# Scores of two heads in one task, FFN tiles moved by 32 bytes, warm matmuls in another bank

## The chip, the cores and the metric

The kernel runs on one core of a Trainium2 chip. The metric is the device time of one execution in microseconds (us): the median of three runs.

## The reference

Windowed attention with four sink positions feeds two FFN layers. Shapes: batch 2, 8 heads, 768 tokens, head size 64; the FFNs map 1536 tokens of width 512 through 2048 hidden columns and back.

```
scores = q @ k.T / sqrt(64)
keep   = (key < n_sink) | (0 <= query - key < window)      # n_sink = 4, window = 128
a      = softmax(where(keep, scores, -1e9))
x      = (a @ v), heads side by side -> (1536, 512)
h = x @ w1_in;  g = h if h >= 1, 0 if h <= -1, else (h + 1)**2 / 4;  x = g @ w1_out
h = x @ w2_in;  out = relu(h)**2 @ w2_out
```

The inputs arrive as 64-bit numbers; the output is float32.

## The kernel before

**Attention** is cut into 24 units (`UNITS`): batch b, block j of 256 queries, pair c of two heads. The name of a tile carries them: `s_0_2_1_1_0` is the score tile of unit (b 0, j 2, c 1), query half u = 1, head e = 0. A unit goes through these tasks: `tp` (TensorE turns k and q into bank `tp`) and `tpc` (VectorE copies them to `k`), `s` (TensorE: scores of one head and one half, 260 keys wide, 128 in a sequence's first half), `m` (VectorE adds the mask and takes the least, L668, which frees the score bank), `e` (ScalarE's exponential), `n`, `pm`, `sp` (normalizing, VectorE and GpSimd), `x` and `ts` (TensorE turns the weights; ScalarE copies), `av` (TensorE, weights times values), `xh` and `xl` (the result, split in two float32r parts, goes to the big tile `x`).

A score matmul contracts over the 64 rows of one head: head 0 uses rows 0 to 63 of TensorE, head 1 rows 64 to 127. The scores have two PSUM banks (`SCB = 2`), one tile each.

**The FFN** works in passes over chunks of 128 hidden columns. Weights come from HBM by SyncE's queue, are split in two float32r parts by ScalarE, VectorE and GpSimd (`wx`, `wy`, `w`), and lie in nine slots of 8 KB per partition: slots 0 to 5 stand on the left side of SBUF, beside `x`; slots 6 to 8 stand on the right side and open when attention is over. Chunks take the slots in turn. A hidden step is twelve matmuls (L357, tile `h`, moving operand `x`, stationary `w`), an output step is three matmuls for each chunk of the pass (L425, tile `o`; in the first FFN `g` moves and `w` is stationary, in the second `w` moves and `g` is stationary). A piece of 256 tokens is taken while attention still runs (`STEPS`, passes 0 and 1), one of 512 later. The later `g` tiles are on the right side too.

**Places.** `fill` puts a tile in front of the FFN's tiles so that they start at a multiple of `LINE` = 2048 bytes. It reckons with `BOTTOM`, the bytes that the pools `one` and `first` take. They take 11,328 bytes, and `BOTTOM` says 11,296: so the left tiles stand 32 bytes behind a multiple of 2048 (the built program has `x` at byte 61,472 and weight slot 0 at 12,320). The right side's weight slots and `g` tiles stand at multiples of 512 (slot 6 at 219,136).

**The order** of all instructions from the fast path on is a list made when the kernel is built: `Planner.run` takes the task that can start first by its table of costs, and among those that can start at once the one with the least key (`KEYS`, `STEPS`, `LOADS`, `PARTS`). Each engine works through its part of the list in order. Where the planner leaves TensorE idle before the first FFN matmul, `warm_gaps` puts matmuls of the identity (`warm_c`). `warm_pe` does the same by hand at the start: `warm_a`, `warm_b` and `warm_d`, around the sum that spreads the parameters over the partitions (`par_ps`, L233, bank `psf0`), whose copy is `par_all` (L241).

Of the kernel before, what the change touches and what calls it, by code (L numbers as in the profile page):

```python
# [8 lines left out]
F32 = mybir.dt.float32  # L9
# [8 lines left out]
P = 128  # L18
# [10 lines left out]
SCALE = 0.125  # L29
BIG = 8.0e9  # L30
GRP = 2
WARM = 3, 3, 1
VB, KB = 5, 6
PB, PTB = 6, 4
WR = 2
UNITS = [(b, j, c) for b in range(B) for j in range(3) for c in range(NC)]
RING, EARLY = 9, 6
G0, G1 = 7, 6
LINE, BOTTOM, TOP, DMA_SCRATCH = 2048, 11296, 229344, 1024
PSF, SCB, TPB, TXB = 2, 2, 1, 2  # L40
HALF = 256
SLOTS = dict(
    q=2, v=VB, k=KB, p=PB, pt=PTB, sm=4, sp=2, st=2, vs=1, av=2, sc=SCB, tp=TPB, tx=TXB, f=PSF,
# [1 line left out]
)  # L45
LATE = dict(f=8 - PSF, w=RING - EARLY, G=G1, U=2, T=2)
KEYS = dict(
    q=-82.12, v=149.88, kd=-59.27, kp=-207.24, tp=115.34, tpc=40.08, kp0=-0.30, s0=1.56,
    m0=-62.00, e0=130.89, s1=2.49, m1=-159.82, e1=180.50, n=27.64, pm0=296.62, sp0=-106.62,
    pm1=-268.00, sp1=11.63, x0=-230.35, xc0=-85.23, x1=-6.43, xc1=106.04, ts=-154.44, tsc=122.15,  # L50
    tsl=3.21, av=207.79, xh=-0.06, xl=-291.84, vs=94.69, vc=-27.99, k1=102.40, k2=-128.71,
)
STEPS = [
    (0, 0, 157.84), (0, 256, -39.25), (0, 512, 13.62), (1, 512, 52.44), (0, 1024, -5.62),
    (1, 0, 59.36), (1, 256, 63.06), (1, 1024, 135.44), (0, 768, 23.61), (1, 768, 394.12),
    (0, 1280, 34.67), (1, 1280, 129.91),
]
SPREAD = 21.09, 3.72
LOADS = [-36.47, 48.25, 302.68, -2.39, -160.55, 14.45]
PARTS = [170.15, 9.91, -52.22, 170.63, -252.48, 135.47]  # L60
START = dict(SP=4900.0, PE=6500.0, ACT=6900.0, DVE=5900.0, POOL=5700.0)
LEAD = 153.00, 55.20
LAG = dict(PE=53, ACT=33, DVE=33, POOL=78, SP=40)
COST = dict(
    q=("SP", 2200, 0, 2320), v=("SP", 1100, 0, 1160), kd=("SP", 500, 0, 230), wi=("SP", 500, 0, 1470),
# [2 lines left out]
    pm=("POOL", 1012, 1060, 0), pms=("POOL", 562, 615, 0), sp=("POOL", 139, 203, 0),  # L68
    cl=("POOL", 1235, 1275, 0), gl=("POOL", 690, 740, 0), gl5=("POOL", 1240, 1290, 0),
    yl=("POOL", 690, 740, 0), yl5=("POOL", 1240, 1290, 0),  # L70
    tp=("PE", 436, 620, 0), s=("PE", 320, 389, 0), ss=("PE", 207, 285, 0), x=("PE", 436, 633, 0),
    xx=("PE", 327, 490, 0), ts=("PE", 218, 400, 0), av=("PE", 1230, 1390, 0), avv=("PE", 790, 870, 0),
    mm=("PE", 120, 283, 0), mm5=("PE", 226.7, 390, 0),
    e=("ACT", 500, 510, 0), es=("ACT", 392, 400, 0), xc=("ACT", 492, 587, 0), xxc=("ACT", 375, 478, 0),
# [44 lines left out]
class Planner:  # L119
# [28 lines left out]
    def switch(self, last, t):  # L148
        if last is None or t.engine != "PE":
            return 0.0  # L150
        if t.kind in ("s", "ss"):
            return 0.0 if last.kind in ("s", "ss") else 90.0
        if last.kind in TURNS:
            return 50.0 if t.kind in TURNS else -80.0
        return 0.0
# [407 lines left out]
class Attention:  # L563
# [84 lines left out]
            blocks = slice(4 * i // len(ps), 4 * (i + 1) // len(ps))  # L648
            copy(self.kt[b, j, c][:, 1:, :P][:, blocks], ps[i][:, blocks])  # L649

    def scores(self, b, j, c, u, e):
        nc, po, st = self.nc, self.po, self.st[b, j, c]
        kt = self.kt[b, j, c]
        keys = kt.rearrange("p n w -> p (n w)")
        k0 = SLOT if (j == 0 or u == 1) else 0
        wid = P if j + u == 0 else WIN
        ps = st["s", u, e] = po["sc"].tile([P, 512], F32, tag="s", name=f"s_{st['nm']}_{u}_{e}")[:, :wid]
        pr = slice(64 * e, 64 * e + 64)
        nc.tensor.matmul(ps, kt[pr, 3 + u, :P], keys[pr, k0 : k0 + wid], start=True, stop=True)  # L659

    def least(self, b, j, c, u, e):
        nc, po, st = self.nc, self.po, self.st[b, j, c]
# [101 lines left out]
    def plan(self, line):  # L764
        add, hold = line.add, Hold
        raw, val, keyh, sinks, self.mask_tasks = {}, {}, {}, {}, {}
        u = {}
        for n, unit in enumerate(UNITS):
            b, j, c = unit
            old = u.get((b, j - 1, c))  # L770
            d = u[unit] = {}
            at = lambda f, *a, t=unit: (lambda: f(*t, *a))
            key = lambda nm, n=n: n + KEYS[nm]
            if (j, c) == (0, 0):
                h, sinks[b, 0] = hold("pt"), hold("vs")
                uses = ([h], []), ([], []), ([sinks[b, 0]], []), ([], []), ([], [h])
                last = None
                for i, (kind, f) in enumerate(self.sinks(b)):
                    at0 = n + KEYS["vs"] if i < 2 else n + KEYS["vc"] + 0.01 * i
                    last = add(kind, at0, f, [last], *uses[i])  # L780
                sinks[b] = last
            g = (b, j, c // 2)
            if c % 2 == 0:
                if n:
                    raw[g] = hold("q")
                    d["q"] = add("q", key("q"), at(self.loads.load, "qk"), takes=[raw[g]])
                val[g] = hold("v")
                d["v"] = add("v", key("v"), at(self.loads.load, "v"), takes=[val[g]])
            else:
                d["q"], d["v"] = u[b, j, c - 1].get("q"), u[b, j, c - 1]["v"]  # L790
            kt = keyh[unit] = hold("k")
            if j > 0:
                d["kd"] = add(
                    "kd", key("kd"), at(self.keys_load), [old["tpc"]], [kt], [keyh[b, j - 1, c]]
                )
                d["kp"] = add(
                    "kp", key("kp"), at(self.keys_sink), [d["kd"], old["kp"]], [], [keyh[b, j - 1, c], kt]
                )
            if n:
                h = hold("tp")  # L800
                t = add("tp", key("tp"), at(self.turn), [d["q"]], [h], [raw[g]] if g in raw else [])
                d["tpc"] = add(
                    "tpc", key("tpc"), at(self.turn_copy), [t], [] if j else [kt], [h, kt],
                    behind=d.get("kd"),
                )
            else:
                kt.pool = "none"
                d["tpc"] = None
            if j == 0:
                d["kp"] = add("kp0", key("kp0"), at(self.keys_sink), [d["tpc"]], [], [kt])  # L810
            ph, sm, exps = [hold("p"), hold("p")], hold("sm"), []
            for i in range(2):
                small = "s" if j + i == 0 else ""
                for e in range(2):
                    least = None if i + e == 0 else least
                    h = hold("sc")
                    t = add(
                        "s" + small, key(f"s{i}") + 0.001 * e, at(self.scores, i, e),
                        [d["tpc"], d["kp"], d.get("kd")], [h], [kt],
                    )  # L820
                    t = add(
                        "m" + small, key(f"m{i}") + 0.001 * e, at(self.least, i, e),
                        [t, self.mask_of(line, min(2 * j + i, 2))], [ph[i]] * (e == 0) + [sm] * (i + e == 0),
                        [h], behind=least,
                    )
                    least = t
                    exps.append(add("e" + small, key(f"e{i}") + 0.001 * e, at(self.powers, i, e), [t]))
            norm = add("n", key("n"), at(self.norm), exps)
            pm, cols = [], []
            sp, stt, av = hold("sp"), hold("st"), hold("av")  # L830
            for i in range(2):
                small = "s" if j + i == 0 else ""
                pm.append(add("pm" + small, key(f"pm{i}"), at(self.weigh, i), [norm], [], [sm]))
                if j > 0:
                    cols.append(
                        add("sp", key(f"sp{i}"), at(self.sink_cols, i), [pm[-1]], [sp][i:], [ph[i]])
                    )
            turned, ptu = [], []
            few = "x" if j == 0 else ""
            for e in range(2):  # L840
                h, pt = hold("tx"), hold("pt")
                t = add(few + "x", key(f"x{e}"), at(self.turn_p, e), pm, [h], ph)
                turned.append(add(few + "xc", key(f"xc{e}"), at(self.turn_p_copy, e), [t], [pt], [h]))
                ptu.append(pt)
            if j > 0:
                h = hold("tx")
                t = add("ts", key("ts"), at(self.turn_s), cols, [h], [sp])
                t = add("tsc", key("tsc"), at(self.turn_s_copy), [t], [stt], [h])
                turned.append(add("tsl", key("tsl"), at(self.turn_s_low), [t], [], [h]))
# [378 lines left out]
def attention_ffn_kernel(ctx, tc, q, k, v, n_sink, window, w1i, w1o, w2i, w2o, out):  # L1228
    nc = tc.nc
# [14 lines left out]
    with tc.manual_schedule(engines={mybir.EngineType.DVE, mybir.EngineType.PE}):  # L1244
# [3 lines left out]
        masks = Masks(nc, one, par)  # L1248
        par.compute(psf[0], masks.m[2][0:1, :P])
        masks.begin()  # L1250
        warm_pe(nc, ident, psf, "b", WARM[1])
        at.turn(*UNITS[0])
        at.turn_copy(*UNITS[0])
        masks.first()
# [40 lines left out]
```

## Time and profile before

| | |
|---|---|
| median of three runs | 671.44 us (670.66 to 671.64) |
| the profiled execution | 671.85 us |
| its span, first to last instruction | 670.1 us |
| TensorE busy | 655.4 us, 98% |
| VectorE, ScalarE, GpSimd busy | 438.6, 331.1, 299.7 us |
| mean granted TensorE clock | 0.994 |

The profiled execution takes 1.75 us more than its span. Attention's last matmuls run at about 178 us; from there to the end there is FFN alone. TensorE counts as busy from a matmul's start to its modelled end, with the ends of neighbours overlapping, so 98% busy does not say that nothing is lost.

### The profile page before, as it was taken

What the parts mean: (1) busy time and instruction counts of PE and PEld (TensorE: products, weight loads), DVE (VectorE), ACT (ScalarE), POOL (GpSimd) and SP (SyncE); (2) the same over time, 40 slices, a digit from 0 to 9 for tenths busy, and PEclk for the clock granted to TensorE, in tenths of its full rate; (3) what the DMA queues carried; (4) which work ended last, traced back from release to release, by engine and by line L of the source; (5) the groups of instructions that cost most, each with busy time, mean ns of one, the idle gap of its engine ahead of it and who ended that gap; (6) DMA issues with size and microseconds to landing.
All of it is one profiled execution on the core that took longest, in us unless ns stands there. A gap on an engine that the chain in (4) does not pass through costs nothing.

```text
span 670.1 us, 9926 instructions
## 1 busy us (share of the span) xinstructions
PE 655.4 (98%) x3550; PEld 536.8 (80%) x3550; DVE 438.6 (65%) x906; ACT 331.1 (49%) x720; POOL 299.7 (45%) x314
## 2 busy tenths in 40 slices
PE   8998999989999999999999999999999999999997
PEld 6575777878999988888888888888888888888885
DVE  4877899876668587676777687666666566622222
ACT  3777877865455444344445555533544444412220
POOL 3447565556144253344444697433543444323311
PEclk9998999999999999999999999999999999999999
DMA  6664641211021123221121122222212211100011
GB/s 150 170 155 110 146 131 41 81 63 33 3 93 64 33 64 94 64 64 63 64 81 50 58 64 64 63 64 69 88 63 72 86 64 64 32 1 31 32 63 70
DMA packets 63904, 47.95 MB, mean 72 GB/s; under 512 B 39652, under 2 KB 58340, under 8 KB 63844
## 3 DMA queue, kind: packets, MB, share of 16 engines
q1 hardware_dynamic: 62466, 46.56, 23.8%
q10 hardware_dynamic: 1378, 0.66, 0.3%
q8 instruction: 30, 0.49, 0.3%
q14 instruction: 30, 0.25, 0.1%
HBM read 43.01 MB, written 3.15 MB: 69 GB/s over the span
## 4 chain that ended last, share of the span: by engine, by line
PE 95%; DVE 2%; ACT 1%; issue 1%; POOL 0%; POOLq 0%; DVEq 0%
PE h L357 40%; PE o L425 40%; PE s L659 5%; PE av L747 3%; PE tx L706 3%; PE tp L635 2%; DVE p L668 1%; PE warm_c L866 1%; PE ts L719 1%; DVE k L649 1%; ACT p L676 0%; ACT pt L713 0%; PE warm_b L866 0%; PE warm_a L866 0%; DVE wx L299 0%
## 5 line engine op out<-in xcount | busy, mean ns | idle before, releaser
L357 PE MATMUL h<-x,w 128*128 128x512 f32 (+1 forms) x1368 | 279.1, 359 | 0.2 <-DVE acc L462 0.2
L357 PEld LDWEIGHTS h<-x,w 128*128 128x128 f32 x1368 | 229.7, 189 | 41.5 <-DVE t L371 0.8
L301 POOL TENSOR_TENSOR w<-wx,w 128x512 fp32r<-128x512 f32 x64 | 83.4, 1303 | 146.7 <-ACT w L300 134.1
L425 PE MATMUL o<-g,w 128*128 128x256 f32 (+1 forms) x792 | 142.5, 335 | 1.2 <-DVE acc L462 1.2
L425 PEld LDWEIGHTS o<-g,w 128*128 128x128 f32 x792 | 120.7, 190 | 19.4 <-DVE acc L462 2.3
L425 PE MATMUL o<-w,g 128*128 128x512 f32 (+1 forms) x588 | 135.6, 389 | 0.0
L425 PEld LDWEIGHTS o<-w,g 128*128 128x128 f32 x588 | 108.8, 188 | 25.1
L382 POOL TENSOR_TENSOR g<-t,g 128x512 fp32r<-128x512 f32 x48 | 63.7, 1327 | 91.3 <-ACT g L378 65.9
L382 POOL TENSOR_TENSOR g<-u,g 128x256 fp32r<-128x256 f32 (+1 forms) x66 | 71.7, 1092 | 70.0 <-ACT g L378 61.8
L464 DVE TENSOR_TENSOR acc<-o,acc 128x512 f32<-128x512 f32 (+1 forms) x109 | 59.8, 563 | 62.4 <-PE o L425 62.2
L373 DVE SCALAR_TENSOR_TENSOR t<-h,u 128x512 f32<-128x512 f32 x48 | 33.1, 689 | 71.4 <-ACT u L366 43.1
L300 ACT CAST w<-wx 128x512 fp32r<-128x512 f32 x64 | 39.8, 621 | 79.2 <-DVE wx L299 79.1
L371 DVE SCALAR_TENSOR_TENSOR t<-u 128x256 f32<-128x256 f32 (+1 forms) x66 | 46.7, 708 | 27.8 <-ACT u L364 27.4
L690 POOL TENSOR_TENSOR p<-p,sm 128x520 f32<-128x520 f32 (+1 forms) x48 | 49.1, 1034 | 33.1 <-DVE sm L683 19.2
L289 DVE SCALAR_TENSOR_TENSOR wx<-wraw,wx 128x512 int32<-128x512 int32 x64 | 62.4, 975 | 1.3
L279 ACT ACTIVATE wx<-wraw 128x512 f32<-128x512 f32 x64 | 42.7, 667 | 38.1 <-POOL w L301 38.0
L364 ACT ACTIVATE u<-h,half 128x256 f32<-128x256 f32 (+1 forms) x66 | 37.3, 569 | 47.3 <-PE h L357 38.3
L366 ACT ACTIVATE u<-h 128x512 f32<-128x512 f32 x48 | 28.5, 594 | 52.9 <-PE h L357 50.9
L676 ACT ACTIVATE p<-p,sm 128x260 f32<-128x260 f32 (+1 forms) x96 | 46.7, 488 | 14.2 <-DVE sm L668 13.9
L299 DVE CUSTOM_DVE_ANT_0 wx<-wx,wy 128x1024 uint16<-128x1024 uint16 x64 | 50.6, 790 | 2.3
L378 ACT CAST g<-u 128x256 fp32r<-128x256 f32 (+1 forms) x66 | 32.7, 501 | 29.5 <-DVE u L389 19.7
L659 PE MATMUL s<-k 64*128 64x260 f32 (+1 forms) x192 | 42.2, 437 | 4.9 <-DVE sm L668 4.8
(79 smaller groups left out, 574.1 us busy)
## 6 DMA issues: line engine op xcount, KB each, us to landing
wraw<-in_moe_w_in_dram SPq DMA_DIRECT2D x32, 512.0 KB, 3.8
wraw<-in_moe_w_out_dram SPq DMA_DIRECT2D x32, 512.0 KB, 3.2
vr<-in_v_dram SPq DMA_DIRECT2D x24, 128.0 KB, 2.7
qr<-in_q_dram SPq DMA_DIRECT2D x22, 128.0 KB, 2.5
kr<-in_k_dram SPq DMA_DIRECT2D x22, 128.0 KB, 3.1
out_dram<-acc SPq DMA_DIRECT2D x10, 256.0 KB, 2.1
k<-k SPq DMA_DIRECT2D x16, 64.0 KB, 2.3
qr<-in_q_dram SPq DMA_DIRECT2D x4, 64.0 KB, 2.4
```

The source lines that it names most:

```text
L279: nc.scalar.activation(s["x"], f32(s["r"][:, :, 1]), AF.Abs, scale=65536.0)
L289: nc.vector.scalar_tensor_tensor(s["xi"], s["r"][:, :, 1], -(1 << 31), s["xi"], ALU.bitwise_and, ALU.bitwise_or)
L299: ("c4", lambda: nc.vector.tensor_tensor(s["xi"], s["xi"], s["yi"], ALU.add)),
L301: ("cl", lambda: nc.gpsimd.tensor_tensor(s["w"][:, 1], s["x"], f32(s["w"][:, 0]), ALU.subtract)),
L357: nc.tensor.matmul(s["h"], w[:, a, c * P : (c + 1) * P], x[:, b, c, sl], start=n == 0, stop=n == 11)
L371: nc.vector.scalar_tensor_tensor(t, s["u"], 1.0, s["u"], ALU.min, ALU.mult)
L382: nc.gpsimd.tensor_tensor(g[:, 1], s["u" if ffn == 0 else "t"], f32(g[:, 0]), ALU.subtract)
L425: nc.tensor.matmul(s["o"], lhs, rhs, start=n + i + j == 0, stop=n == len(chunks) - 1 and i == 1)
L464: self.nc.vector.tensor_tensor(dst, o, dst, ALU.add)
L659: nc.tensor.matmul(ps, kt[pr, 3 + u, :P], keys[pr, k0 : k0 + wid], start=True, stop=True)
L676: self.nc.scalar.activation(s, s, AF.Exp, bias=sm[:, 0, u, e : e + 1], scale=-1.0, accum_out=sm[:, 1, u, e : e + 1])
L690: self.nc.gpsimd.tensor_tensor(s, s, r, ALU.mult)
```

## The change

Four things are changed. The scores of both heads of a query half are one task, which takes both score banks at once. `BOTTOM` is 11,328, so that the left FFN tiles move 32 bytes down, to multiples of 2048 (`x` to 61,440, slot 0 to 12,288). The matmuls `warm_b` write `psf[1:]`, so bank `psf1` alone, and `WARM` has one less of them and one more `warm_d`. All keys of the planner are other numbers, and the score's cost is that of two.

```diff
-WARM = 3, 3, 1
+WARM = 3, 2, 2
-LINE, BOTTOM, TOP, DMA_SCRATCH = 2048, 11296, 229344, 1024
+LINE, BOTTOM, TOP, DMA_SCRATCH = 2048, 11328, 229344, 1024
-    q=-82.12, v=149.88, kd=-59.27, kp=-207.24, tp=115.34, tpc=40.08, kp0=-0.30, s0=1.56,
+    q=-128.99, v=155.46, kd=-117.16, kp=-232.79, tp=110.17, tpc=65.09, kp0=31.66, s0=-3.92,
...
-    (0, 0, 157.84), (0, 256, -39.25), (0, 512, 13.62), (1, 512, 52.44), (0, 1024, -5.62),
+    (0, 0, 100.20), (0, 256, -58.54), (0, 512, 27.88), (1, 512, 156.32), (1, 0, 42.56),
...
-    tp=("PE", 436, 620, 0), s=("PE", 320, 389, 0), ss=("PE", 207, 285, 0), x=("PE", 436, 633, 0),
+    tp=("PE", 436, 620, 0), s=("PE", 640, 709, 0), ss=("PE", 415, 492, 0), x=("PE", 436, 633, 0),
...
-    def scores(self, b, j, c, u, e):
+    def scores(self, b, j, c, u):
...
-        ps = st["s", u, e] = po["sc"].tile([P, 512], F32, tag="s", name=f"s_{st['nm']}_{u}_{e}")[:, :wid]
-        pr = slice(64 * e, 64 * e + 64)
-        nc.tensor.matmul(ps, kt[pr, 3 + u, :P], keys[pr, k0 : k0 + wid], start=True, stop=True)
+        for e in range(2):
+            ps = po["sc"].tile([P, 512], F32, tag="s", name=f"s_{st['nm']}_{u}_{e}")[:, :wid]
+            st["s", u, e] = ps
+            pr = slice(64 * e, 64 * e + 64)
+            nc.tensor.matmul(ps, kt[pr, 3 + u, :P], keys[pr, k0 : k0 + wid], start=True, stop=True)
...
-                for e in range(2):
-                    least = None if i + e == 0 else least
-                    h = hold("sc")
-                    t = add(
-                        "s" + small, key(f"s{i}") + 0.001 * e, at(self.scores, i, e),
-                        [d["tpc"], d["kp"], d.get("kd")], [h], [kt],
-                    )
+                hs = [hold("sc"), hold("sc")]
+                first = add(
+                    "s" + small, key(f"s{i}"), at(self.scores, i),
+                    [d["tpc"], d["kp"] if j + i else None, d.get("kd")], hs, [kt],
+                )
+                for e, h in enumerate(hs):
...
-        warm_pe(nc, ident, psf, "b", WARM[1])
+        warm_pe(nc, ident, psf[1:], "b", WARM[1])
```

On TensorE, at the program's start, the rows of before, with the semaphores that each waits for (DVE is VectorE, DMAHW a load's landing, PE TensorE's own):

```order
L233 MATMUL par_ps_112<-par_val_110,mask2_102 128x2 [waits DVE_49,PE_49]
L866 MATMUL warm_b_0_125<-ident_67 128x128 [waits DVE_49]
L866 MATMUL warm_b_1_127<-ident_67 128x128
L866 MATMUL warm_b_2_129<-ident_67 128x128 [waits PE_49]
L635 MATMUL tp_0_0_0_0_131<-ident_67,kr_0_0_0_78 128x128 [waits DMAHW3_49,PE_49]
```

and of the change:

```order
L233 MATMUL par_ps_112<-par_val_110,mask2_102 128x2 [waits DVE_49,PE_49]
L867 MATMUL warm_b_0_125<-ident_67 128x128
L867 MATMUL warm_b_1_127<-ident_67 128x128 [waits PE_49]
L635 MATMUL tp_0_0_0_0_129<-ident_67,kr_0_0_0_78 128x128 [waits DMAHW3_49,DVE_49]
L635 MATMUL tp_0_0_0_0_129<-ident_67,kr_0_0_0_78 128x128 [waits DMAHW5_49]
```

The first `warm_b` no longer waits for VectorE's copy, and the first `tp` no longer waits for the warm matmuls' writes.

On TensorE, in the third block of queries of batch 0, the rows of before from the last score of unit (0, 1, 3) on:

```order
L659 MATMUL s_0_1_3_1_1_849<-k_0_1_3_446 128x260
L659 MATMUL s_0_2_0_0_0_851<-k_0_2_0_536 128x260
L659 MATMUL s_0_2_0_0_1_861<-k_0_2_0_536 128x260
L659 MATMUL s_0_2_0_1_0_865<-k_0_2_0_536 128x260
L635 MATMUL tp_1_0_1_0_871<-ident_67,kr_1_0_0_659 128x128 x2
L635 MATMUL tp_1_0_1_0_871<-ident_67,qr_1_0_0_656 128x128 x2
L659 MATMUL s_0_2_0_1_1_882<-k_0_2_0_536 128x260
L659 MATMUL s_0_2_1_0_0_893<-k_0_2_1_547 128x260
L659 MATMUL s_0_2_1_0_1_902<-k_0_2_1_547 128x260
L659 MATMUL s_0_2_1_1_0_906<-k_0_2_1_547 128x260
```

and of the change, from the first score of unit (0, 2, 0) on:

```order
L661 MATMUL s_0_2_0_0_0_865<-k_0_2_0_499 128x260
L661 MATMUL s_0_2_0_0_1_867<-k_0_2_0_499 128x260
L708 MATMUL tx_0_1_2_1_873<-ident_67,p_0_1_2_0_701 128x128 x2
L708 MATMUL tx_0_1_2_1_873<-ident_67,p_0_1_2_1_732 128x128 x2
L661 MATMUL s_0_2_0_1_0_888<-k_0_2_0_499 128x260
L661 MATMUL s_0_2_0_1_1_890<-k_0_2_0_499 128x260
L749 MATMUL av_261<-sink_t0_264,vs_0_438 128x256
```

Scores now stand in pairs of heads of the same half, with turns, `av` and FFN steps (`h_0_0_1`, twelve matmuls, two pairs further down) between the pairs; before, four scores of two different pairs follow each other.

## Rows read from the trace of the kernel before

**Rows 1.** The page: TensorE's busy time, and the chain that ended last, by engine.

```profile
PE   655.4 (98%) x3550; PEld 536.8 (80%) x3550; DVE 438.6 (65%) x906; ACT 331.1 (49%) x720; POOL 299.7 (45%) x314
PE 95%; DVE 2%; ACT 1%; issue 1%; POOL 0%; POOLq 0%; DVEq 0%
```

**Rows 2.** Stretches of attention: busy us (instructions) by engine, granted clock, DMA.

```profile
16.40:41.70 25.30, 23.64 (x171) 16.10 (x171) 19.51 (x70) 19.43 (x62) 12.70 (x24) 1.00 0.75 183
41.70:60.80 19.10, 17.23 (x112) 11.29 (x111) 16.18 (x55) 15.18 (x47) 11.12 (x20) 1.00 0.51 130
60.80:67.70 6.90, 6.90 (x34) 5.24 (x33) 3.25 (x9) 3.39 (x10) 5.29 (x8) 0.51 0.18 42
67.70:120.00 52.30, 50.39 (x396) 39.54 (x395) 47.52 (x146) 40.92 (x123) 30.06 (x43) 1.00 0.42 110
120.00:180.00 60.00, 58.10 (x469) 49.35 (x468) 42.77 (x119) 39.11 (x104) 28.93 (x39) 1.00 0.14 41
```

**Rows 3.** The chain in order of time, second FFN: start us, us, what.

```profile
466.21 10.89 PE h L357 x48
477.10 11.19 PE o L425 x48
...
576.78 11.13 PE h L357 x48
587.91 11.04 PE o L425 x48
```

**Rows 4.** Groups by line and shape: FFN matmuls 512 wide, count, busy us, mean ns.

```profile
L357 PE MATMUL h<-x,w 128*128 128x512 f32 x936 | 219.4, 391 | 0.0
L425 PE MATMUL o<-w,g 128*128 128x512 f32 x564 | 132.8, 394 | 0.0
L425 PE MATMUL o<-g,w 128*128 128x512 f32 x360 | 85.9, 394 | 0.0
```

**Rows 5.** TensorE, program start: start us, us, line, tile, records [idle before].

```profile
3.41 0.58 PE L233 MATMUL par_ps<-par_val,mask 1*128 1x2 f32 x2
4.25 1.65 PE L866 MATMUL warm_b<-ident 128*128 128x128 f32 x6 [0.25 <-DVE par_all L241]
5.96 0.69 PE L635 MATMUL tp<-ident,kr 128*128 128x128 f32 x2
...
7.98 0.80 PE L659 MATMUL s<-k 64*128 64x128 f32 x4
```

**Rows 6.** Line L659, the scores: what ended idle time before them (us, times).

```profile
  DVE sm L668: 13.5, 26
```

**Rows 7.** TensorE in order of time: a pair of heads alone, then two pairs running.

```profile
69.01 0.71 PE L659 MATMUL s<-k 64*128 64x260 f32 x4
69.65 0.38 PE L747 MATMUL av<-sink_t,vs 96*128 96x256 f32 x1
...
143.51 0.71 PE L659 MATMUL s<-k 64*128 64x260 f32 x4
144.75 1.05 PE L659 MATMUL s<-k 64*128 64x260 f32 x4 [0.52 <-DVE sm L668]
145.73 0.39 PE L747 MATMUL av<-sink_t,vs 96*128 96x256 f32 x1
```

**Rows 8.** TensorE in order of time, 50 to 66 us: the third block's scores.

```profile
50.92 1.05 PE L659 MATMUL s<-k 64*128 64x260 f32 x4 [0.52 <-DVE sm L668]
...
55.33 0.70 PE L659 MATMUL s<-k 64*128 64x260 f32 x2
55.96 1.09 PE L706 MATMUL tx<-ident,p 128*128 128x128 f32 x8
...
60.58 1.58 PE L659 MATMUL s<-k 64*128 64x260 f32 x4 [0.68 <-DVE sm L668]
62.09 1.11 PE L706 MATMUL tx<-ident,p 128*128 128x128 f32 x4
...
65.57 1.63 PE L357 MATMUL h<-x,w 128*128 128x256 f32 x6
```

More of the change, by code (lines that the diff above doesn't have):

```diff
@@ L47 @@
 KEYS = dict(
-    q=-82.12, v=149.88, kd=-59.27, kp=-207.24, tp=115.34, tpc=40.08, kp0=-0.30, s0=1.56,
-    m0=-62.00, e0=130.89, s1=2.49, m1=-159.82, e1=180.50, n=27.64, pm0=296.62, sp0=-106.62,
-    pm1=-268.00, sp1=11.63, x0=-230.35, xc0=-85.23, x1=-6.43, xc1=106.04, ts=-154.44, tsc=122.15,
-    tsl=3.21, av=207.79, xh=-0.06, xl=-291.84, vs=94.69, vc=-27.99, k1=102.40, k2=-128.71,
+    q=-128.99, v=155.46, kd=-117.16, kp=-232.79, tp=110.17, tpc=65.09, kp0=31.66, s0=-3.92,
+    m0=-102.11, e0=252.45, s1=-3.31, m1=-67.76, e1=276.89, n=56.38, pm0=592.38, sp0=-61.87,
+    pm1=-212.96, sp1=89.25, x0=-220.28, xc0=-249.08, x1=-19.51, xc1=50.14, ts=-99.41, tsc=98.15,
+    tsl=42.27, av=248.63, xh=6.01, xl=-352.66, vs=28.63, vc=-54.27, k1=-185.94, k2=-176.52,
 )
 STEPS = [
-    (0, 0, 157.84), (0, 256, -39.25), (0, 512, 13.62), (1, 512, 52.44), (0, 1024, -5.62),
-    (1, 0, 59.36), (1, 256, 63.06), (1, 1024, 135.44), (0, 768, 23.61), (1, 768, 394.12),
-    (0, 1280, 34.67), (1, 1280, 129.91),
-]
[L58 to L62, printed above, removed]
+    (0, 0, 100.20), (0, 256, -58.54), (0, 512, 27.88), (1, 512, 156.32), (1, 0, 42.56),
+    (0, 1024, 124.89), (1, 256, 68.66), (1, 1024, 281.52), (0, 768, -15.98), (1, 768, 400.16),
+    (0, 1280, -3.57), (1, 1280, 161.21),
+]
+SPREAD = 26.48, 15.61
+LOADS = [13.24, -77.84, 364.45, -42.84, -98.01, -150.31]
+PARTS = [78.66, 20.27, -1.00, 151.41, -446.58, 123.12]
+START = dict(SP=4100.0, PE=6400.0, ACT=6400.0, DVE=5950.0, POOL=6500.0)
+LEAD = 197.30, 93.66
 LAG = dict(PE=53, ACT=33, DVE=33, POOL=78, SP=40)
@@ L151, in switch @@
         if t.kind in ("s", "ss"):
-            return 0.0 if last.kind in ("s", "ss") else 90.0
+            return 0.0 if last.kind in ("s", "ss") else 95.0
         if last.kind in TURNS:
@@ L810, in plan @@
                 d["kp"] = add("kp0", key("kp0"), at(self.keys_sink), [d["tpc"]], [], [kt])
-            ph, sm, exps = [hold("p"), hold("p")], hold("sm"), []
+            ph, sm, exps, least = [hold("p"), hold("p")], hold("sm"), [], None
             for i in range(2):
                 small = "s" if j + i == 0 else ""
-                for e in range(2):
-                    least = None if i + e == 0 else least
-                    h = hold("sc")
-                    t = add(
-                        "s" + small, key(f"s{i}") + 0.001 * e, at(self.scores, i, e),
-                        [d["tpc"], d["kp"], d.get("kd")], [h], [kt],
-                    )
+                hs = [hold("sc"), hold("sc")]
[4 more added lines that the diff above has]
+                for e, h in enumerate(hs):
                     t = add(
                         "m" + small, key(f"m{i}") + 0.001 * e, at(self.least, i, e),
-                        [t, self.mask_of(line, min(2 * j + i, 2))], [ph[i]] * (e == 0) + [sm] * (i + e == 0),
-                        [h], behind=least,
+                        [first, self.mask_of(line, min(2 * j + i, 2))],
+                        [ph[i]] * (e == 0) + [sm] * (i + e == 0), [h], behind=least,
                     )
```

## Prediction

> **What bounds the kernel now.** I read the page first. TensorE is busy for 655.4 us and makes up 95% of the chain that ended last [rows 1], so the time is TensorE's work plus what TensorE loses. I then looked for the loss by stretches and found two kinds. In attention, up to 180 us, the engines take turns in waiting: from 41.7 to 60.8 us VectorE is busy for 16.18 of 19.1 us and from 67.7 to 120 us for 47.52 of 52.3 us, and TensorE's own busy share there hides waits, because a score that runs alone counts as busy like a full matmul [rows 2]. Scores waited 13.5 us in 26 places for VectorE's `m` to free a bank [rows 6]. From 180 us on there is no wait at all, and the loss is in the pace of the matmuls: 48 hidden matmuls of 512 columns take 10.89 us in one step and 11.13 in another, 48 output matmuls 11.19 and 11.04 [rows 3]. So the second loss is small for each matmul, but there are 936 + 564 + 360 = 1860 of that width [rows 4].
>
> **The 32 bytes.** The pace follows the places. The step at 466.21 us belongs to chunks 4 to 7 of the second FFN. All their weights are in left slots, 32 bytes off, like `x`. Its hidden matmuls have moving and stationary operand off by the same amount: 10.89 / 48 = 226.9 ns each. Its output matmuls stream left weights over a right `g`, 32 against 0: 11.19 / 48 = 233.1 ns. At 576.78 us it is chunks 8 to 11, three right, one left. Now hidden is the mixed one (36 of 48) and takes 11.13, and output, with 12 of 48 mixed, falls to 11.04 [rows 3]. The slow matmuls change sides with the slot, so neither the line nor the tile explains them. I read it as the stationary operand's load, which runs during the matmul before it, getting in the way of the moving one when the two differ by 32 bytes modulo 64; equal is fast, whether 0 or 32.
>
> How many are mixed: slots go in turn, so the right ones hold chunks 6, 7, 8, 15 of the first FFN and 0, 1, 8, 9, 10 of the second. Hidden: 9 chunks x 3 pieces x 12 = 324. Output of the first FFN (`g` right, weights left): chunks 9 to 14, 6 x 36 = 216. Of the second: 11 left chunks x 36 = 396, less 12 that are issued in halves, 384. Sum 924 of 1860. Afterwards none is. The price of one has these bounds: (11.19 - 11.04) / 36 = 4.2 ns, which gives 3.9 us; (11.19 - 10.89) / 48 = 6.25 ns, 5.8 us; and if all 1860 came to the pace of the best step, the two pairs of steps lose 0.30 and 0.39 us in 96 matmuls, 3.6 ns each on average, 6.7 us in all. **I take 6.0 us**, near the middle value, because matched output matmuls in a step with mixed ones are a little slow too. The 256-wide pieces during attention use left tiles on both sides and change nothing.
>
> The Trainium skill speaks against this part. TensorE: Matmul & The Clock Gate, "Step-by-step: what each phase is for", says that the engine has two independent read ports: "Loading the next tile's weights doesn't steal SBUF read bandwidth from the running matmul." By that rule the 6.0 us would be zero. The rows at 466.21 and 576.78 us do not agree with it, as far as my reading of the places is right.
>
> **The start.** Before, `par_ps` begins at 3.41 us, `warm_b` waits 0.25 us for VectorE's copy, begins at 4.25 and takes 1.65 us for three matmuls (six records), and `tp` begins at 5.96, behind their last write [rows 5]. In the change nothing stands between: 0.58 us for `par_ps` and four sixths of 1.65 for two matmuls put `tp` at 3.41 + 0.58 + 1.10 = 5.1 us, 0.87 earlier. Of this the extra `warm_d` may take back up to 0.3 to 0.4 us (a matmul of two records) before the first score at 7.98. What follows is a chain of ScalarE, VectorE and TensorE without slack, so the shift is kept. **I take 0.6 us**, with 0 (a load or the masks come last) and 1.2 (records of warm matmuls overlap more than their 1.65 us says) as bounds. Three more `warm_c` (12 for 9) fill planned idle time of TensorE; their cover is the wait for VectorE, and without it they would cost a matmul each, about 0.4 us at that place, 1.2 us.
>
> **The scores and the new order.** A pair whose heads start together takes 69.65 - 69.01 = 0.64 us [rows 7]; one head alone takes 55.96 - 55.33 = 0.63 us [rows 8]. Two heads at once cost what one costs. Before, 11 of the 48 pairs are split by other work, and in 15 places a pair follows a score directly. There the first head starts when one bank is free and the second 0.35 us later: two such pairs take 145.73 - 143.51 = 2.22 us in place of 1.28, a loss of 0.94 us [rows 7]. The change has no split pair and no such place. Its price is that a pair waits for both banks, and TensorE's queue stands behind it: with less than 0.94 us of other work since the last pair, TensorE idles for the rest. By the new order that is so for nine pairs from the third unit on, 0.22 to 0.87 us of work in front of each, 4.3 us missing in all.
>
> From 67.7 us on FFN work is there and TensorE is the limit: four places of 0.94 us go, 3.8, and five short pairs come, 2.7: a gain of 1.1. From 41.7 to 60.8 us eight places go; but VectorE has as much to do as before, and only 19.1 - 16.18 = 2.9 us of it are free [rows 2], of which I take half, 1.5. Right behind, from 60.8 to 67.7, the clock was granted at 0.51, its lower level of 1.2 GHz [rows 2], after ten microseconds of single heads and waits of up to 0.68 us [rows 8]; TensorE then worked without a gap until `h` at 65.57, so that stretch lost up to 6.9 x 0.49 = 3.4 us. The new order puts turns, `av` and an FFN step into those waits, but other thin places arise; I count a quarter, 0.8. From 16.4 to 41.7 I count nothing. **Sum 3.4 us.** Bounds: all 15 places gained against the short pairs, 14.1 - 4.3, and the clock too, if VectorE's share moves elsewhere, would be over 10, of which I hold 9 possible; on the other side nine pairs that each wait the 0.35 us for the second bank with nothing gained, a loss of 3.2 us.
>
> **Sum.** The profiled execution took 671.85 us, its span of 670.1 and 1.75 around it: 671.85 - 6.0 - 0.6 - 3.4 = 661.85 us. It was 0.41 above the median of the runs; I forecast **661.4 us** for the median.
>
> **Rivals.**
> 1. Pace and start gain, but the new order gains nothing, because VectorE and ScalarE bind attention: 671.44 - 6.6 = 664.8 us. For it speaks VectorE's 47.52 of 52.3 us; against it, the idle time before scores.
> 2. The places have no part in the pace (the rule above): 671.44 - 4.0 = 667.4 us. Against it stands the swap of sides in rows 3.
> 3. Slower: every pair holds TensorE's queue until the second bank is free, 0.35 us x 48 = 16.8 us, and no gap is filled: 671.44 - 6.6 + 16.8 = 681.6 us. It decides from 0.14 us for each pair on (6.6 / 48). Against it: 39 of 48 pairs have 0.94 us of other work in front.
> 4. The low clock stretch goes and the waits do: 9 us in attention, 655.8 us.
>
> **How the numbers follow.** Chances: the forecast 0.48, rival 1 0.28, rival 2 0.10, rival 3 0.07, rival 4 0.07. The low end takes most of rival 4 away, the high end takes in rivals 1 and 2 with 3.9 us for the pace: 656 to 668 us. A measurement of this kernel tells a change of about 0.2%, 1.3 us. Slower is rival 3, 0.07; same is rival 2 without a gain in attention, 0.04; all else is faster, 0.89.
>
> **What would show it.** Right, if every late step of 48 matmuls takes 10.9 us, hidden and output alike; if the first score starts near 7.4 us; if scores always start in pairs a few ns apart, and the last `av` is followed by an end that is earlier by more than the pace's 6 us. The prediction is wrong if output steps stay at 11.1 to 11.2 us, if a wait for VectorE in front of the scores adds up to more than 13.5 us, or if the clock falls to its lower level over a longer stretch. SyncE's order moved too: the values `vr` of the third block's second pairs now stand behind the weights `wraw_1_1`, which wait for a raw slot; an `av` that waits for that load would add to the loss.

## The result and the profile after

The changed kernel takes 653.16 us (median of four runs, 652.9 to 654.08), against 671.05 in four runs of before: a ratio of 0.9747, 95% interval 0.9711 to 0.9783. It is faster, as forecast, but by 18 us and not by 10, and outside the range that was given (656 to 668).

The profiled execution took 654.08 us, its span is 652.1. To see where the 17.77 us between the two profiled executions lie I take a place at which both orders have done the same work: the first matmul of `h_0_768_0`, ahead of which 540 FFN matmuls and all of attention stand in both. It starts at 194.47 us before and at 183.12 after, so 11.35 us come from ahead of it. From it to the last matmul 470.46 us became 463.53, 6.93 less. The end behind the last matmul and around the span is 0.5 us longer.

Behind that place first. The page's engine line answers to [rows 1]:

```profile
PE 640.4 (98%) x3556; PEld 531.3 (81%) x3556; DVE 437.5 (67%) x906; ACT 331.1 (51%) x720; POOL 299.7 (46%) x314
```

The chain in order of time, second FFN (start us, us, what), answers to [rows 3]:

```profile
450.79 10.88 PE h L357 x48
461.67 10.88 PE o L425 x48
...
516.23 10.88 PE h L357 x48
527.11 10.88 PE o L425 x48
```

Hidden and output steps of 48 now take the same 10.88 us, whichever slots their weights are in (one output step, at 505.19 us, takes 11.03): the steps that took 11.04 to 11.19 have come down to the best pace. The groups by shape, answering to [rows 4], say it for all 1860:

```profile
L357 PE MATMUL h<-x,w 128*128 128x512 f32 x936 | 216.9, 389 | 0.0
L425 PE MATMUL o<-w,g 128*128 128x512 f32 x564 | 129.9, 389 | 0.0
L425 PE MATMUL o<-g,w 128*128 128x512 f32 x360 | 84.3, 389 | 0.0
```

219.4 + 132.8 + 85.9 us of busy time became 216.9 + 129.9 + 84.3: 7.0 less. Taken one by one from the trace, each from its start to the next start, 1082 of the 1860 take 230 ns or more before, 233.3 on average, and nearly all others 226.7; in the changed kernel 24 do.

Now ahead of it. The stretches of attention, answering to [rows 2] (busy us and instructions by engine in the order PE, PEld, DVE, ACT, POOL; then granted clock and DMA):

```profile
16.40:41.70 25.30, 23.89 (x182) 16.85 (x182) 23.70 (x79) 20.96 (x66) 14.02 (x25) 1.00 0.81 202
41.70:60.80 19.10, 17.64 (x128) 11.27 (x128) 18.11 (x58) 17.38 (x53) 12.67 (x21) 1.00 0.55 140
60.80:67.70 6.90, 6.59 (x50) 4.46 (x49) 6.39 (x25) 5.94 (x21) 5.24 (x10) 1.00 0.51 112
```

VectorE is the engine to look at. From 16.4 to 41.7 us it works 23.70 us where it worked 19.51, from 41.7 to 60.8 it works 18.11 for 16.18, from 60.8 to 67.7 it works 6.39 for 3.25. By 67.7 us it has done some 9 us more of its work, of which about 1.5 go with an early full pace at the start that is told of below. The stretch at half the granted clock (0.51 before) is gone.

The scores' line (idle time before them, us and times, by what ended it) answers to [rows 6]:

```profile
  issue: 4.6, 24
  DVE sm L670: 3.0, 11
```

13.5 us in 26 places became 3.0 in 11. This view adds up the waits of the score matmuls (4.8 us in 10 places before, 0.8 in 3 after) and those of their weight loads (8.7 in 16, 2.2 in 8), which can run side by side; so TensorE's matmuls never stood still for 13.5 us.

What the scores take of TensorE is seen best if each matmul's time is counted from its start to the next one's start, and added by tile up to `h_0_768_0`, so that the sum is the whole time. (The third column is a run of the changed kernel's order that comes to full pace late; it is told of below.)

| us, start to next start | before | after | after's order, late pace, old warm matmuls |
|---|---|---|---|
| scores `s` | 45.41 | 34.95 | 35.68 |
| values `av` | 29.49 | 27.50 | 27.50 |
| turns `tp`, `tx`, `ts` | 38.81 | 38.99 | 39.50 |
| FFN | 69.97 | 70.17 | 70.20 |
| warm matmuls, `par_ps` | 9.08 | 9.80 | 11.01 |
| ahead of the first | 1.71 | 1.72 | 1.72 |
| sum | 194.47 | 183.12 | 185.61 |

The gain of attention is nearly all in one row. The scores give 10.5 us and `av` gives 2.0, 1.1 of which come as well where the low clock alone is taken away (e10, below).

### The profile page after: what moved, and what is told of

Its sections match the earlier page's. It is cut to its first block, busy times and chain, and to the rows that moved or that the text cites. A ratio compares the mean times of both kernels' runs of the same rounds, so it can differ in the third digit from the quotient of the medians.

```text
span 652.1 us, 9933 instructions
## 1 busy us (share of the span) xinstructions
PE 640.4 (98%) x3556; PEld 531.3 (81%) x3556; DVE 437.5 (67%) x906; ACT 331.1 (51%) x720; POOL 299.7 (46%) x314
## 4 chain that ended last, share of the span: by engine, by line
PE 90%; DVE 4%; ACT 2%; POOL 1%; issue 1%; DMA 0%; SPq 0%; POOLq 0%; DVEq 0%
PE o L425 41%; PE h L357 39%; PE s L661 3%; PE av L749 3%; PE tx L708 2%; PE tp L635 1%; DVE p L670 1%; ACT p L678 1%; POOL p L692 1%; ACT pt L715 0%; PE ts L721 0%; DVE sm L684 0%; DVE x L759 0%; DMA vr<-in_v_dram 0%; DVE k L649 0%
## 5 line engine op out<-in xcount | busy, mean ns | idle before, releaser
L357 PE MATMUL h<-x,w 128*128 128x512 f32 (+1 forms) x1368 | 275.3, 357 | 0.0
L425 PE MATMUL o<-w,g 128*128 128x512 f32 (+1 forms) x588 | 132.8, 385 | 0.0
L382 POOL TENSOR_TENSOR g<-u,g 128x256 fp32r<-128x256 f32 (+1 forms) x66 | 70.3, 1071 | 56.0 <-ACT g L378 51.8
L371 DVE SCALAR_TENSOR_TENSOR t<-u 128x256 f32<-128x256 f32 (+1 forms) x66 | 45.0, 683 | 25.1 <-ACT u L364 24.5
L678 ACT ACTIVATE p<-p,sm 128x260 f32<-128x260 f32 (+1 forms) x96 | 46.9, 491 | 16.8 <-DVE sm L670 16.7
L296 DVE TENSOR_SCALAR wx<-wx 128x512 f32<-128x512 f32 x64 | 37.2, 581 | 13.3 <-ACT wx L279 13.2
```

The costliest lines, as they stand in the source:

```text
L357: nc.tensor.matmul(s["h"], w[:, a, c * P : (c + 1) * P], x[:, b, c, sl], start=n == 0, stop=n == 11)
L371: nc.vector.scalar_tensor_tensor(t, s["u"], 1.0, s["u"], ALU.min, ALU.mult)
L382: nc.gpsimd.tensor_tensor(g[:, 1], s["u" if ffn == 0 else "t"], f32(g[:, 0]), ALU.subtract)
L425: nc.tensor.matmul(s["o"], lhs, rhs, start=n + i + j == 0, stop=n == len(chunks) - 1 and i == 1)
L678: self.nc.scalar.activation(s, s, AF.Exp, bias=sm[:, 0, u, e : e + 1], scale=-1.0, accum_out=sm[:, 1, u, e : e + 1])
```

## The experiments

Theory: three things add up, each worth its size alone. The places set the pace of the late matmuls (7 us), heads that start together save TensorE what a second head costs (about 9 us), and the start gives the rest. Rivals: the keys of the planner, not the pairs, make the gain; the clock makes it; the places have no part.

### The places

Six kernels move tiles and nothing else; the order of instructions stays that of the kernel that they are made from. The edit is one line, for e1:

```diff
-LINE, BOTTOM, TOP, DMA_SCRATCH = 2048, 11296, 229344, 1024
+LINE, BOTTOM, TOP, DMA_SCRATCH = 2048, 11328, 229344, 1024
```

| | made from | `BOTTOM`, `TOP` | left and right tiles modulo 256 | us, median |
|---|---|---|---|---|
| e1 | before | 11328, 229344 | 0, 0 | 664.08 |
| e5 | before | 11296, 229312 | 32, 32 | 663.96 |
| e7 | after | 11296, 229344 | 32, 0 | 662.24 |
| e6 | after | 11392, 229344 | 192, 0 (64 below a multiple) | 660.04 |
| f2 | after | 11456, 229344 | 128, 0 | 660.49 |
| f1 | after | 11584, 229344 | 0, 0 (256 below a multiple of 2048) | 653.96 |

e1. 

> The kernel before with the left tiles at multiples of 2048 bytes and nothing else. From the milestone h_0_768_0 on the changed kernel was 6.9 us shorter. Theory (the places set the pace): 671 - 7 = 664 us, hidden and output steps of 48 both at 10.88 us, attention up to h_0_768_0 as before, at 194 us. Rival (the pace came from other work beside it, or from the new order): 671 us, output steps stay at 11.2.

664.08 us (663.92 to 664.15) against 671.23, ratio 0.9893 (0.9878 to 0.9908). The places alone give 7.15 us.

e5. 

> The kernel before with its left tiles where they were, 32 bytes off, and the right weights and g moved by 32 bytes as well, so that every moving and stationary operand is 32 modulo 64 and none lies at a multiple of 64. Theory (only the difference modulo 64 counts): as e1, 664 us. Rival (a tile off the multiples of 64 is slow whatever the other is): all 1860 wide matmuls slow, 6.6 ns more for the 936 that were fast, 671 + 6 = 677 us.

663.96 us, ratio 0.9890 (0.9875 to 0.9905). The chain of this kernel, where every tile is 32 bytes off:

```profile
483.21 10.88 PE h L357 x48
494.09 10.88 PE o L425 x48
```

So no place is slow by itself; two operands must differ. Which two, before's own trace shows. In the step at 466.21 us the hidden matmuls take 226 or 227 ns to the next start, but the last of them, behind which an output matmul loads a right `g`, takes 235. The output matmuls behind it take 231 to 235, but the last of them, behind which a left weight is loaded, 227. It is the stationary operand of the next matmul that counts, not a matmul's own. The Trainium skill's rule that was weighed in the prediction (TensorE: Matmul & The Clock Gate, "Step-by-step: what each phase is for": the next tile's load does not take read bandwidth from the running matmul) would have made these places worth nothing. The runs do not agree: only addresses changed, and the time fell by 7 us. That it is read bandwidth which is lost they do not show.

e7. 

> The changed kernel with its left tiles back at 32 bytes off, the order of instructions the same on every engine. Theory (the places cost 7 us in either order): 653.2 + 7 = 660 us, all of it behind h_0_768_0. Rival (the two parts help each other, since TensorE has less slack now): 656 or 664 us.

662.24 us (662.18 to 662.28), ratio to before 0.9866 (0.9851 to 0.9881). Between the profiled executions it is 8.1 us above the changed kernel. Of these 1.7 lie ahead of `h_0_768_0` (184.78 us for 183.12), where the moved tiles are not yet in use when the difference arises; they are a subject of the start below. Behind it 470.44 us stand against 463.53, 6.9 more, as in before's order; the end is 0.5 us shorter. The two parts of the change add up.

e6. 

> The changed kernel with its left tiles 64 bytes below the multiples of 2048 (448 modulo 512 against 0 on the right), the order the same. Theory (the difference modulo 64 alone counts): steps of 48 at 10.88 us as in the changed kernel, 653.2 us, or 655 where the full pace at the start comes late. Rival (the tiles must lie at multiples of 512 or 2048 bytes): as the run with the tiles back at 32 off, 660 to 662 us.

660.04 us (659.05 to 660.32): slow, and my theory of 64 bytes is wrong. The chain has the swap of sides again, first with all weights left, then with three of four right:

```profile
487.22 11.20 PE o L425 x48
498.42 10.91 PE h L357 x48
...
542.70 11.15 PE h L357 x48
553.85 11.04 PE o L425 x48
```

f2. 

> The changed kernel with its left tiles 128 bytes below the multiples of 2048, the order the same. If the period is 128 bytes: 653 to 655 us, all steps of 48 at 10.88. If it is longer: 660 to 662 us, mixed steps at 11.2.

f1. 

> The changed kernel with its left tiles 256 bytes below the multiples of 2048, the order the same. If the period is 256 bytes or less: steps of 48 at 10.88 us, 653 to 655 us. If operands must be equal modulo 512: mixed steps at 11.2 us, 660 to 662 us.

128 bytes apart is slow, 660.49 us (659.99 to 662.46); 256 is fast, 653.96 (653.87 to 655.22). Their chains at the same two steps, f2 and then f1:

```profile
487.71 11.16 PE o L425 x48
498.87 10.89 PE h L357 x48
```

```profile
483.45 10.88 PE o L425 x48
494.33 10.88 PE h L357 x48
```

Differences of 32, 64 and 128 bytes between the moving operand and the next stationary one cost about 6 to 7 ns in a matmul of 227; differences of 0 and 256 cost nothing. The period is 256 bytes, as far as these five distances tell. 2048, the change's number, is a multiple of it; multiples of 256 would have done.

### Pairs or keys

e3 has the pairs as one task, with their costs and the three lines that go with them, and before's keys, warm matmuls and places.

e3. 

> The kernel before with the pairs as one task and their costs, but the keys, start values and warm matmuls of before, and the places of before. Theory (the scores were what TensorE lost, 10.5 us over the 192 records): most of the gain of attention comes with the pairs whatever the keys, 671 - 8 = 663 us (660 to 666), scores take some 35 us to the next matmul in place of 45. Rival (the gain is in the keys, which were found for this order): 669 to 675 us.

683.98 us (682.5 to 684.54), ratio 1.0182 (1.0167 to 1.0198): slower by 12.8 us, and the rival seems right. The trace tells more. Its 541st FFN matmul, the place of `h_0_768_0` in the other orders, starts at 191.15 us, 3.3 ahead of before, although five pairs stand in one row at 119 to 126 us, with a stretch of low clock (0.83 on average from 120 to 140 us) around them. But 2.2 us of turns and values still stand behind that matmul here, so little more than 1 us is gained. The loss comes later. The waits from 180 us on (us, times, longest), and the windows there:

```profile
PE h L357 <- ACT w L300: 7.2, 1, 7.2
```

```profile
120.00:140.00 20.00, 18.23 (x109) 12.32 (x110) 16.62 (x60) 16.78 (x51) 12.11 (x18) 0.83 0.19 60
...
240.00:250.00 10.00, 3.54 (x19) 2.65 (x17) 7.01 (x12) 4.17 (x7) 3.24 (x3) 0.85 0.25 87
250.00:260.00 10.00, 9.15 (x26) 6.87 (x27) 3.64 (x7) 4.16 (x7) 2.95 (x3) 0.64 0.33 107
```

At 244 us a chunk of weights is not ready: its decoding begins only at 246 us, behind the previous step's activation, and I put that down to the old keys. TensorE waits 7.2 us and then gets a clock of 0.64 on average. The pairs and the keys can't be judged apart in this way, if each set of keys fits one set of tasks. So the next two kernels keep the changed kernel's order and keys and take only the pairs apart: head 1 of a pair is issued behind the next piece of other work on TensorE, in every fourth pair or in all 48.

```diff
+        if t.kind in ("s", "ss"):
+            n_s += 1
...
+            if n_s % APART == 0:
+                out.append((t.heads[0], False))
+                pend, owner = t.heads[1], t
+                continue
...
+        if pend and t.engine == "PE":
+            out.append((pend, False))
```

e9, every fourth. 

> The changed kernel, its order kept, but in every fourth pair (12 of 48) the second head is issued behind the next piece of other work on TensorE. Theory (two heads started together cost what one costs, so a split pair adds up to 0.63 us to TensorE): 12 times 0.3 to 0.63, 657 to 661 us. Rival (the gain of the new order has nothing to do with heads that start together): 653 to 654 us.

e9b, all. 

> As the run before, with all 48 pairs split. Theory: 48 times 0.3 to 0.63 us, 668 to 683 us, the scores take some 58 us to the next matmul in place of 35. Rival: 653 to 656 us.

665.25 us (663.4 to 667.69) and 687.64 (684.44 to 690.06), both above what the theory gave at most. By the profiled executions, 663.4 and 687.67 against 654.08, a split pair costs 0.78 us with 12 of them (1.0 by the medians) and 0.70 with 48 (where a stretch of low clock between 76 and 92 us is among it). That is more than the 0.63 us that one head takes; that what follows the second head is late as well is my reading. The scores' groups up to 210 us (busy us, mean ns, idle before), of before, after, e9 and e9b in this order, each from its own trace:

```profile
L659 PE MATMUL s<-k 64*128 64x260 f32 (+1 forms) x192 | 42.2, 437 | 4.9 <-DVE sm L668 4.8
```

```profile
L661 PE MATMUL s<-k 64*128 64x260 f32 (+1 forms) x192 | 35.1, 422 | 1.0 <-DVE sm L670 0.8
```

```profile
L662 PE MATMUL s<-k 64*128 64x260 f32 (+1 forms) x192 | 43.0, 422 | 1.4 <-DVE sm L671 1.3
```

```profile
L662 PE MATMUL s<-k 64*128 64x260 f32 (+1 forms) x192 | 61.2, 445 | 0.4 <-DVE sm L671 0.4
```

Busy and idle together make 47.1 us before, 36.1 after, 44.4 and 61.6 with pairs split. The means of one record hardly differ, 422 to 445 ns: what changes is how many of them run side by side. This is the experiment that changes the pairs alone.

Its price can't be carried over to the 11 split pairs of before, as before's trace shows. Each score's records counted from start to next start, the pairs of before are of three kinds:

| | pairs | us in all | us for one |
|---|---|---|---|
| before, split | 11 | 10.45 | 0.95 |
| before, whole, directly behind another score | 9 | 11.83 | 1.31 |
| before, the others | 28 | 23.11 | 0.83 |
| after, all | 48 | 34.92 | 0.73 |

Against 0.73 us for each, the split pairs give 2.4 us, the nine 5.3 and the others 2.7 (a wait between two scores counts with the first). A split pair is cheap in before because its head often runs beside a head of another pair, as the score at 49.69 us does, 7 ns ahead of the first score of the next unit; in e9 most take 1.27, two heads alone.

### The low clock

e10 is the kernel before with a warm matmul ahead of each of 18 score heads between 45 and 62 us.

```diff
+        steps += t.kind == "mm"
+        if t.kind in ("s", "ss") and steps == 2:
+            emit = lambda n=len(out): warm_pe(nc, ident, psf, f"f{n}", 1)
+            out.append((emit, False))
```

> The kernel before with one warm matmul of 128 columns ahead of each of the 18 score heads between 45 and 62 us, where TensorE waits for banks; nothing else. Theory (the low clock from 60.8 us is a cost of its own, up to 3.4 us, and goes if TensorE has work in the waits): no stretch at the lower level, 671.1 - 2 to 3.4 = 668 to 669 us. Rival (what the clock costs there is hidden behind VectorE): 670.5 to 671.5 us; or the warm matmuls delay the scores by 0.2 us each, 672 to 675 us.

676.43 us (676.16 to 677.28), ratio 1.0084 (1.0071 to 1.0098). The low clock is gone, and it is slower all the same:

```profile
41.70:60.80 19.10, 19.06 (x119) 13.03 (x116) 12.21 (x39) 11.66 (x34) 7.95 (x15) 1.00 0.39 100
60.80:67.70 6.90, 6.90 (x36) 4.34 (x34) 4.30 (x16) 5.36 (x18) 3.42 (x6) 1.00 0.30 88
```

To `h_0_768_0` the warm matmuls take 16.03 us in place of 9.08; `av`, the turns `tx` and the FFN give 2.2 back, the turns `tp` and the scores take 1.0 more (full pace comes at 19.3 us here, 16.5 in before, which is told of below), and the sum is 5.5 us worse. The waits before the scores were not free time: with each score delayed, VectorE falls from 16.18 us of work to 12.21 in the same stretch. So a wait before a score is no free place for other work: what is put there delays the loop between TensorE and VectorE. That this delay is the whole of the loss is not shown.

The clock's price is seen more cleanly in the executions of before itself, over all rounds. Ten of them have a mean granted clock of 0.994, like the profiled one with its 6.8 us at half the clock; they took 671.71 to 671.93 us. Eight have 0.999 or 1.000, too much for such a stretch, and took 670.34 to 670.62. So the low clock costs about 1.3 us there (3.4 was my upper bound).

### The start

Five kernels change the warm matmuls alone. The edit of e2 is:

```diff
-WARM = 3, 3, 1
+WARM = 3, 2, 2
...
-        warm_pe(nc, ident, psf, "b", WARM[1])
+        warm_pe(nc, ident, psf[1:], "b", WARM[1])
```

e8 is the changed kernel with this edit undone; f3 and g2 are the changed kernel with `WARM = 3, 1, 2`, f4 with `3, 2, 1`, and g1 with `3, 1, 1`.

e2. 

> The kernel before with the warm matmuls of the change alone (two in place of three ahead of the transposes, on the other bank, two behind). Theory (clock): transposes 0.6 us earlier, and the engine comes to full pace earlier than 16.4 us, near 11.5 as in the changed kernel; 1 to 2.5 us less, 669.3. Rival (the start is bound by the chain of VectorE and ScalarE): 0.3 us less or nothing, 671.

670.64 us (669.33 to 671.53), ratio 0.9989 (0.9980 to 0.9998). The first score starts at 7.62 us for 7.98, but full pace comes at 16.8 (16.5 before), and the ninth `m` starts at 19.16 for 19.18: in these two profiles the shift is gone by then. The low clock behind it lasts 3.4 us for 6.8. That is not the whole of the half microsecond in the median, for at the same mean clock of 0.994 e2 took 671.26 to 671.53 us and before, beside it, 671.71 to 671.85.

e8. 

> The changed kernel with the warm matmuls of before (three ahead of the transposes on both banks, one behind), the order otherwise the same on every engine. Theory (the start is a shift that is mostly lost again, as the run with the warm matmuls alone showed, and full pace near 11.5 us comes from the order): 653.2 + 0.5 = 653.7 us, full pace still near 11.5 us. Rival (the warm matmuls bring the early full pace): full pace near 16.5 us and 1.5 to 2.5 us more, 655.5 us.

656.09 us (653.99 to 656.72), with full pace at 17.7 us. That is what the rival gave, but not for its reason. (Full pace is where the trace's record of the granted clock begins, at 1.00, the 2.4 GHz level; 128-column matmuls that follow each other 213 ns apart ahead of it are about 110 apart behind it. Ahead of it the trace has no record of the clock, and the view prints 1.00 there too.) Here the profile must be read beside e7's, which has the changed kernel's warm matmuls. TensorE in order of time in the changed kernel (start us, us, what):

```profile
3.42 0.58 PE L233 MATMUL par_ps<-par_val,mask 1*128 1x2 f32 x2
3.93 1.65 PE L867 MATMUL warm_b<-ident 128*128 128x128 f32 x4
5.38 0.63 PE L635 MATMUL tp<-ident,kr 128*128 128x128 f32 x2
...
7.63 0.80 PE L661 MATMUL s<-k 64*128 64x128 f32 x4
...
10.57 1.34 PE L867 MATMUL warm_c<-ident 128*128 128x128 f32 x6
11.84 0.49 PE L661 MATMUL s<-k 64*128 64x128 f32 x4
12.26 0.49 PE L867 MATMUL warm_c<-ident 128*128 128x128 f32 x2
```

And in e7, the same instructions in the same order with tiles of the FFN elsewhere, which no matmul uses before 32 us:

```profile
10.57 1.65 PE L867 MATMUL warm_c<-ident 128*128 128x128 f32 x6
12.15 0.80 PE L661 MATMUL s<-k 64*128 64x128 f32 x4
12.88 0.79 PE L867 MATMUL warm_c<-ident 128*128 128x128 f32 x2
```

Up to 11.37 us all TensorE starts of the two agree within 1 ns. Then one kernel's `warm_c` follow each other in 121 and 144 ns where they took 213, and the other's go on at 213 until 16.5 us. From the ninth `m` on (16.95 against 18.66) e7 is 1.7 us behind, up to the end of attention. The warm matmuls are the same in both, so they don't make the difference. e8 is another 0.83 us behind e7 at `h_0_768_0`, but that is not the price of its warm matmuls, for its full pace comes 1.2 us later than e7's. The changed kernel itself, in two executions told of below, has full pace at 16.6 and at 18.0 us and is at 184.83 and 185.55 there, about 0.5 us for one. At 17.7 us it would be at some 185.4, and e8 is at 185.61. As an estimate from these four, the warm matmuls are worth some 0.2 us in this order.

after_again. 

> The changed kernel once more, unchanged, beside the others. If the early full pace at 11.4 us belongs to it: all runs within 652.9 to 654.1 us. If it is chance: some runs 1.7 us longer, near 655.

653.95 us (653.84 to 655.36); its profiled execution is the 655.36 and comes to full pace at 16.6 us. So the same kernel has both, and the 652.9 to 654.1 of the first four runs are not all that it shows.

f3. 

> The changed kernel with one warm matmul in place of two ahead of the first transposes. If the start is bound by them: transposes 0.5 us earlier, first score near 7.1 us, and 0.4 to 0.8 us less, 652.7 us where full pace comes early. Rival: loads, masks or the branch come last, no change, 653.2 to 654; and if a busy TensorE at the start brings the early pace, late pace in more of the runs, 655.

f4. 

> The changed kernel with one warm matmul in place of two ahead of the first score. If the first score waits for them (it starts behind the last one, 0.8 us after the copies of the keys): first score near 7.2 us, 0.3 us less, 652.9. Rival: no change, 653.2 to 654, or late pace in more of the runs, 655.

653.21 us (652.24 to 654.14) and 654.08 (653.5 to 655.09). First scores start at 6.77 and 7.30 us for 7.63, full pace came early in both profiles (9.4 and 11.2 us for 11.4), and `h_0_768_0` is at 181.84 and 182.82 for 183.12.

g1. 

> The changed kernel with one warm matmul in place of two both ahead of the transposes and ahead of the first score. If both were in the way: first score near 6.4 us, 0.3 us less than with two ahead of the score, 652.9 us. Rival: the copies of the keys or the branch come last, or full pace comes late, 653.5 to 655.

g2. 

> The version with one warm matmul ahead of the transposes again. If the start is bound by it: 0.8 to 1.3 us below the changed kernel in the same call, in runs with the same pace at the start. Rival: the same within 0.3 us.

g3. 

> The changed kernel beside them: 652.9 to 654.1 us where full pace comes early, 655.4 where it comes late.

652.71 us (652.53 to 654.28), 654.29 (654.14 to 655.0) and, for the changed kernel, 655.03 (653.05 to 656.1). In all three profiles full pace came late (15.5, 16.9, 18.0 us), and `h_0_768_0` is at 183.72, 184.55 and 185.55: in order of their first scores, 6.47, 6.77 and 7.63 us, and of their full pace, so that these profiles can't tell the two apart. With one warm matmul less in both places the kernel is 1.8 us below the changed one by these profiles and 2.3 by the medians; single runs of the two overlap. It has the lowest median here, by a margin about as large as what the chance of the pace moves; that it is faster is not shown.

## Why the prediction was right in kind and wrong in size

**The places: right, a little small.** Forecast 6.0 us (3.9 to 6.7), measured 6.93 behind `h_0_768_0` and 7.15 by the medians of e1. The price was right, 6.5 ns for each of 924, where the slow ones take 6.7 more than the others; the count was not, for 1082 are slow. Matched ones in mixed steps are among them, and why is open. The reading that the stationary load of the next matmul meets the moving operand of this one stands in so far as only their difference counts (e5) and the next one's operand is the one that matters (the step at 466.21 us). "By 32 bytes modulo 64" was wrong: it is 256 (e6, f2, f1). For the change both rules say the same, so the sum did not suffer.

**The start: right in sign, and mostly something else.** Forecast 0.6 us. The first `tp` starts at 5.38 us (5.1 was forecast, 5.96 before) and the first score at 7.63 (7.4, 7.98 before). The shift was not kept: up to `h_0_768_0` some 0.2 us of it are left by the estimate above. The other 2.3 of the 2.5 us between e8 and the changed kernel's first profile (185.61 and 183.12) go with the early full pace, which was in no term. I had read full pace at 16.4 us as a fact of the program.

**The new order: the step that failed.** Forecast 3.4 us (a loss of 3.2 to a gain of 9), measured 194.47 - 185.61 = 8.9 between profiles, with the warm matmuls of before and late pace on both sides. By the medians, 671.08 - 656.09 less 6.9 for the places, it is 8.1. The mechanism, two heads for the price of one, was right, and 14.1 us had been worked out for the 15 places. But most of it was given away: "From 16.4 to 41.7 I count nothing", and in the next stretch half of the 2.9 us that VectorE had free, 1.5.

The runs show in its place what each stretch gives. The scores' records in order of time, the same number in both kernels, cost TensorE from start to next start (the last two columns agree, although their pace at the start does not):

| before's stretch | records | before | after | e8 | forecast |
|---|---|---|---|---|---|
| 16.4 to 41.7 us | 40 | 9.61 | 6.70 | 6.70 | no gain |
| 41.7 to 60.8 | 33 | 10.06 | 6.17 | 6.17 | 1.5 less |
| from 67.7 on | 100 | 20.11 | 17.65 | 17.66 | 1.1 less |

So 2.9 us came where nothing was counted, 3.9 where 1.5 were, and 2.5 where 1.1 were. The first had no ground: [rows 2] show VectorE with 5.8 us free there, and after it works 4.2 of them (2.8 in e8). In the second it works 1.9 of its 2.9 free us (1.8 in e8). From 60.8 to 67.7, where the prediction priced the clock alone, VectorE had 3.65 us free and works 3.1 of them. So VectorE's free time held as a bound in every stretch; what failed was to take none or half of it. The 11 split pairs, which the prediction names, stand in no term of its sum; by before's trace they are 2.4 us. (It also has eight places from 41.7 to 60.8 us; by the trace there are seven. No term rests on that.)

**The clock.** I counted a quarter of 3.4 us, 0.8, on its own. The executions of before put it at 1.3, so it was near, and it is a part of the 8.9, since the profiled execution of before is one with the low stretch.

**The price of a pair.** I set 2.7 us for five short pairs late in attention, and rival 3 had TensorE held by every pair. In the changed kernel 39 of the 48 pairs start within 25 ns, the other nine 120 to 350 ns apart; the score matmuls wait 0.8 us for VectorE in 3 places, and their weight loads 2.2 in 8. Rival 3 is ruled out, and so are rival 1 (the order gains) and rival 2 (e1). Rival 4, with a chance of 0.07, came nearest: 655.8 us, with 9 us in attention. The forecast missed because it made little of its own mechanism; the early full pace, which was in no term, moved the result further, and that part is chance.

## What to carry to other kernels

Where an engine hands work to another in a loop and the slower one is busy for 75 to 85%, ask what it waits for in the rest, and count all of that as open to gain: here two thirds or so of it came. Two matmuls on different rows of TensorE cost what one costs (0.64 and 0.63 us) only where both can start at once, so plan them as one task, and expect to set the order's numbers anew for it: with old ones the same pairs made the kernel 13 us slower, a wait of 7 us for a weight among it. Keep the operands that follow each other on TensorE equal modulo 256 bytes where long runs of 512-wide matmuls leave no wait to hide behind.

## What the runs showed that was not expected

A difference of 32, 64 or 128 bytes between moving and next stationary operand costs 6 to 7 ns of 227; 0 and 256 cost none. TensorE's pace at the start rises at 11.4 us in one execution and at 16.6 and 18.0 in others of the same kernel, with starts that agree within 9 ns before it, and 1.7 to 2.4 us of the way to `h_0_768_0` hang on it; what decides between them the runs don't show. The view of the granted clock prints 1.00 ahead of the rise as well, where the trace has no record, so the spacing of matmuls of one kind, 213 against 110 ns, is what tells the level there. A stretch of 6.8 us at half the clock, in the waits of attention, cost before 1.3 us, and filling those waits with other matmuls cost 5.5.
